# Seeding Strassen's second product in PSUM, a subtraction ahead of half of block 0's exponentials, and a new written order

## The chip, the cores and the metric

The kernel runs on one core of a Trainium2 chip. The metric is the device time of one execution in microseconds (us), lower is better. The engines are named as the profile names them: PE (TensorE, matrix products; its weight loads stand apart as PEld), DVE (VectorE), ACT (ScalarE), POOL (GpSimd) and SP (SyncE, which here only issues DMAs).

## The reference

An attention over pooled keys, and then a gated feed-forward layer on its output:

```
# q, k, v: (8, 8, 576, 64); keys and values are means over 8 neighbours, so 72 keys a head
scores = matmul(q, k_p.T) / sqrt(64)
scores = scores - max(scores)
attn   = exp(scores) / (sum(exp(scores)) + 1e-9)
x      = matmul(attn, v_p)  ->  reshaped to (4608, 512)
gate   = 1 / (1 + exp(-(x @ w_gate)))       # w_gate, w_val: (512, 1536)
out    = (gate * (x @ w_val)) @ w_out       # w_out: (1536, 512)
```

All of it is float32, to float32 accuracy.

## The kernel before, in words

The 4608 tokens are nine blocks of 512. A product is made in float32 accuracy from fp32r matmuls: each operand is split into a high and a low part (ACT casts the high part, DVE subtracts it to get the low one), and three matmuls take the place of one.

**Block 0** goes first, alone, in `first_pass`, beside the conversion of the weights (they arrive as float64 and are converted on ACT and DVE) and the attention of blocks 1 and 2. Each step of it is a word of the table `ORDER`; `exp.0.2.1`, for instance, is the exponential of block 0, pair of heads 2, half 1. For a pair and a half, `scores` fills a PSUM tile `sc` (128 queries x 4 x 72 keys), `maximum` takes the negated row maxima on DVE, and `exps` runs four ACT instructions of 72 columns, each with its own row maximum as bias and with a running sum (`accum_out`). The sums give 1/sum (`total`), the weighted values are transposed (tile `tp`), split and multiplied with the values (`av`), and become the operand `xo` of the feed-forward matmuls, whose PSUM tiles are called `chain` (x times w_gate or w_val) and `acc` (h times w_out).

**Blocks 1 to 8** go in four passes of two blocks each. In a pass, both large products use Strassen's method in Winograd's form, seven products m = 1 to 7 in place of eight. `product(kind, p, m)` makes one of them for the gate ("G") or the value ("V") of a pair p of columns: six matmuls of 128x512 into one of three PSUM banks, A, B or C, of that kind. Products 1, 6, 7 and 4 accumulate onto each other in bank A, product 5 and then 3 in bank C, and product 2 stands alone in bank B. After products 1, 5 and 6 ACT copies the bank to SBUF (tiles `sG` and `sV`), and after 2, 3 and 7 DVE adds that copy to the bank (tile `y`): result 0,0 is product 2 plus product 1. The gate's results go through a sigmoid on ACT (tile `gate`); the value's are multiplied with the gate on DVE (tile `h`). `second_sums` does the same for h times w_out with the tiles `acc`, `o` for results. There are 23 pairs in all, each for G and for V, and four second products of two banks each. While a pass multiplies, the attention of the next two blocks runs on the side; blocks 5 to 8 transpose through DRAM by POOL's DMAs (`turned`, `pt`, `pr`).

**The order** of all this is written out. The kernel's calls are only recorded, each as a unit (a group of matmuls that belong together is one unit), and the list `LATER` says in which order all units are issued. Every engine takes its instructions strictly as they stand in that list, so an instruction that waits holds up all that stand behind it on its engine. SP's DMAs have their place in the list too. All recorded instructions carry the line of the one call that issues them (L316), so the profile tells them apart by their tiles.

Of the kernel before, what the change touches and what calls it, by code (L numbers as in the profile page):

```python
# [11 lines left out]
F32 = mybir.dt.float32  # L12
# [3 lines left out]
AF = mybir.ActivationFunctionType  # L16
ALU = mybir.AluOpType
AX = mybir.AxisListType
# [40 lines left out]
BIASED = (3, 4)  # L59
TURNED = {5: ((0, 2), (2, 3), (3, 4)), 6: ((0, 3), (3, 4)), 7: ((0, 3), (3, 4)), 8: ((0, 4),)}  # L60
# [268 lines left out]
def attention_then_ffn(ctx: ExitStack, tc: tile.TileContext, qT, kT, vm, vr, vn, sums8, wgv, wo, const, out, outT):  # L329
# [518 lines left out]


    bank, seen, gates, hb = {}, {}, {}, {}  # L850

    def product(kind, p, m):

        b = {1: "A", 6: "A", 7: "A", 4: "A", 2: "B", 5: "C", 3: "C"}[m]
# [650 lines left out]
```

## Time and profile before

| | |
|---|---|
| time, median of 3 runs | 932.19 us (929.45 to 933.98) |
| the profiled execution | 925.95 us, of which 924.1 us from the first to the last instruction |
| busy in the span | PE 906.7, DVE 689.5, ACT 554.0, POOL 143.3 us |
| weight loads on PE | 741.0 us |
| granted TensorE clock | 0.998 in the mean |

Engines work beside each other, so their busy times don't add up. Only a wait of the engine that is full sets the end. Matmuls are pipelined, and the profile models their ends; a busy PE can hide a short wait. The profiled execution was quicker than the three timed ones.

### The profile page before, as it was taken

To read this page: it belongs to the slowest core of one execution; us is meant where nothing else is said; L and a number is where in the kernel's file an instruction comes from. 1 tells how busy PE (TensorE), PEld (TensorE's weight loads), DVE (VectorE), ACT (ScalarE), POOL (GpSimd) and SP (SyncE) were. 2 spreads that over 40 slices of the span, in tenths; PEclk is the share of its full clock that TensorE was granted. 3 is DMA by queue.
4 is the path that set the end of the run, shared out by engine and by line. 5 is a ranking of instruction groups with operands and counts; after the bars stand their busy time and mean duration, and the time that the engine had idled before them with its cause. 6 is when DMAs were issued, how large, how long until landed. Compare 5 with 4: busy or idle time off the path is not lost.

```text
span 924.1 us, 12611 instructions
## 1 busy us (share of the span) xinstructions
PE 906.7 (98%) x4188; PEld 741.0 (80%) x4188; DVE 689.5 (75%) x1086; ACT 554.0 (60%) x1178; POOL 143.3 (16%) x276
## 2 busy tenths in 40 slices
PE   7999999999999999999999999999999999999998
PEld 5677778878888888887888887888888888888886
DVE  5899989787879999874778988555688773343963
ACT  6999998888786774553546546343455362223442
POOL 1000000011211004424242424213222200000000
PEclk9999999999999999999999999999999999999999
DMA  9798886767785778886977786867646875565454
GB/s 323 268 319 290 296 324 260 257 222 273 286 291 193 254 227 287 264 281 220 329 264 248 232 298 220 265 227 243 225 155 226 246 243 190 205 222 205 172 180 155
DMA packets 96432, 228.38 MB, mean 247 GB/s; under 512 B 12784, under 2 KB 33136, under 8 KB 94832
## 3 DMA queue, kind: packets, MB, share of 16 engines
q1 hardware_dynamic: 83312, 197.68, 62.8%
q0 software_dynamic: 13056, 29.90, 9.7%
q8 instruction: 33, 0.54, 0.2%
q14 instruction: 31, 0.25, 0.1%
HBM read 171.43 MB, written 56.10 MB: 246 GB/s over the span
## 4 chain that ended last, share of the span: by engine, by line
PE 76%; DVE 6%; ACT 4%; DMA 1%; POOL 1%; issue 1%; DVEq 0%; ACTq 0%; SPq 0%; POOLq 0%
PE chain L316 45%; PE acc L316 24%; PE av L316 3%; PE sc L316 3%; POOL turned L316 1%; DVE hs L316 1%; DVE s L316 1%; ACT e L316 1%; DVE xo L316 1%; DMA parts<-keptV0C 1%; DVE h L316 1%; PE tp L316 1%; ACT L316 1%; ACT hs L316 0%; DMA turned<-turn 0%
## 5 line engine op out<-in xcount | busy, mean ns | idle before, releaser
L316 PE MATMUL chain<-xo,parts 128*128 128x512 f32 x2316 | 545.1, 392 | 2.7 <-DVE y L316 1.2
L316 PEld LDWEIGHTS chain<-xo,parts 128*128 128x128 f32 x2316 | 430.5, 188 | 97.1 <-DVE xo L316 2.4
L316 PE MATMUL acc<-hs,oparts 128*128 128x512 f32 x1008 | 238.3, 392 | 0.6 <-DVE hs L316 0.3
L316 PEld LDWEIGHTS acc<-hs,oparts 128*128 128x128 f32 x1008 | 187.3, 188 | 41.6 <-DVE hs L316 2.1
L316 POOL DMA_DIRECT2D turned<-turn x192 | 105.7, 553 | 249.3 <-DVE turn L316 153.6
L316 ACT COPY sG<-chain 128x512 f32<-128x512 f32 x69 | 39.9, 586 | 84.4 <-PE chain L316 84.2
L316 DVE TENSOR_TENSOR y<-chain,sG 128x512 f32<-128x512 f32 x69 | 47.0, 686 | 54.1 <-PE chain L316 32.4
L316 ACT CAST hs<-h 128x1024 fp32r<-128x1024 f32 x52 | 54.5, 1051 | 49.5 <-PE acc L316 39.6
L316 DVE TENSOR_TENSOR y<-chain,sV 128x512 f32<-128x512 f32 x69 | 47.1, 687 | 46.0 <-PE chain L316 31.6
L316 DVE TENSOR_TENSOR hs<-h,hs 128x1024 fp32r<-128x1024 f32 x52 | 63.1, 1218 | 12.1 <-ACT hs L316 11.9
L316 ACT COPY sV<-chain 128x512 f32<-128x512 f32 x69 | 39.7, 584 | 45.0 <-PE chain L316 43.2
L316 ACT CAST hs<-s 128x1024 fp32r<-128x1024 f32 x36 | 37.6, 1051 | 30.3 <-PE acc L316 10.4
L316 ACT ACTIVATE gate<-y 128x512 f32<-128x512 f32 x69 | 43.2, 632 | 17.8 <-DVE y L316 14.7
L316 DVE TENSOR_TENSOR h<-y,gate 128x512 f32<-128x512 f32 x69 | 46.7, 684 | 0.5
L316 DVE TENSOR_TENSOR hs<-s,hs 128x1024 fp32r<-128x1024 f32 x36 | 43.5, 1217 | 4.0 <-ACT hs L316 3.8
L316 ACT ACT_TABLE_LOAD x35 | 44.9, 1283 | 2.1 <-DVE h L316 1.1
L316 PE MATMUL sc<-kbd,raw 128*128 128x144 f32 (+1 forms) x262 | 41.7, 298 | 1.6 <-ACT e L316 1.1
L316 PEld LDWEIGHTS sc<-kbd,raw 128*128 128x128 f32 (+1 forms) x262 | 32.8, 176 | 11.3 <-issue 3.3
L316 PE MATMUL acc<-oparts,hs 128*128 128x512 f32 x144 | 40.9, 413 | 0.1
L316 DVE TENSOR_REDUCE m<-sc 128x4 f32<-128x288 f32 x48 | 21.7, 452 | 15.4 <-PE sc L316 15.2
L316 PEld LDWEIGHTS acc<-oparts,hs 128*128 128x128 f32 x144 | 26.6, 194 | 6.1 <-ACT oparts L316 0.5
L316 DVE TENSOR_TENSOR h<-chain,gate 128x512 f32<-128x512 f32 x23 | 15.8, 687 | 20.0 <-PE chain L316 16.6
(194 smaller groups left out, 1075.8 us busy)
## 6 DMA issues: line engine op xcount, KB each, us to landing
oparts<-keptS SPq DMA_DIRECT2D x48, 512.0 KB, 4.4
oparts<-keptO SPq DMA_DIRECT2D x72, 256.0 KB, 4.5
raw<-in_wgv SPq DMA_DIRECT2D x12, 1024.0 KB, 7.7
out<-o SPq DMA_DIRECT2D x36, 256.0 KB, 3.4
raw<-in_kT SPq DMA_DIRECT2D x28, 288.0 KB, 5.0
raw<-in_qT SPq DMA_DIRECT2D x29, 256.0 KB, 4.3
raw<-in_vm SPq DMA_DIRECT2D x24, 256.0 KB, 4.8
raw_o<-in_wo SPq DMA_DIRECT2D x12, 512.0 KB, 5.8
```

What stands on the lines that cost most here:

```text
L316: return self._book.take(lambda: f(*args, **named))
```

## The change

It has three parts. First, the second Strassen product no longer starts its own bank: after product 1 ACT copies bank A not to SBUF but to bank B, and product 2 accumulates onto that copy. The addition on DVE after product 2 goes away, the sigmoid or the multiplication reads the bank, and in `second_sums` the result of product 2 is copied out by ACT in place of an addition on DVE. Second, for pairs 2 and 3 of block 0 DVE adds the negated row maxima to the scores (288 columns), and ACT then takes one exponential of 576 columns for the pair; DVE sums its rows. Third, `LATER` is a new list.

```diff
+SUBBED = ((0, 2), (0, 3))
...
+    def chain_bank(kind, b):
+        return ps.tile([P, BT], F32, name="chain", tag=CHAIN["GV".index(kind) * 3 + "ABC".index(b)])
+
     def product(kind, p, m):
...
-        if m in (1, 2, 5):
-            bank[kind, b] = ps.tile([P, BT], F32, name="chain", tag=CHAIN["GV".index(kind) * 3 + "ABC".index(b)])
+        if m in (1, 5):
+            bank[kind, b] = chain_bank(kind, b)
...
-                        start=(m in (1, 2, 5) and c == 0 and k == 0), stop=(c == 1 and k == 2), skip_group_check=True,
+                        start=(m in (1, 5) and c == 0 and k == 0), stop=(c == 1 and k == 2), skip_group_check=True,
...
-        if m in (1, 5, 6):
+        if m == 1:
+            bank[kind, "B"] = chain_bank(kind, "B")
+            nc.scalar.copy(bank[kind, "B"], t)
+            return
+        if m in (5, 6):
...
-        if m != 4:
+        if m in (3, 7):
             y = two.tile([P, BT], F32, name="y", tag="y")
-            nc.vector.tensor_tensor(out=y, in0=t, in1=seen[kind, {2: 1, 3: 6, 7: 5}[m]], op=ALU.add)
+            nc.vector.tensor_tensor(out=y, in0=t, in1=seen[kind, {3: 6, 7: 5}[m]], op=ALU.add)
...
-                t = snap.tile([P, BT], F32, name="o", tag=f"sV{5 + c}")
+                t = snap.tile([P, BT], F32, name="o", tag=f"sV{5 + c}" if side else f"s{'GV'[c]}1")
...
-                    if m in (1, 5, 6):
+                    if m == 1:
+                        acc["B", c] = ps.tile([P, BT], F32, name="acc", tag=B_[c])
+                        nc.scalar.copy(acc["B", c], t)
+                    elif m in (5, 6):
...
-                        result(side, half, c, t, None if m == 4 else seen2[{2: 1, 3: 6, 7: 5}[m], c])
+                        result(side, half, c, t, None if m in (2, 4) else seen2[{3: 6, 7: 5}[m], c])
...
         def exps(j, p, hf):
             v = scs[j, p, hf].rearrange("p i (h k) -> p (i h) k", h=2)
+            e = es[p // 2][:, p % 2]
+            if (j, p) in SUBBED:
+                a = slice(QT * hf, QT * hf + QT)
+                m = maxima[j, p][:, a, None].broadcast_to([P, QT, KEYS])
+                nc.vector.tensor_tensor(out=e[:, a], in0=v, in1=m, op=ALU.add)
+                if p in subbed:
+                    nc.scalar.activation(e, e, AF.Exp)
+                    nc.vector.reduce_sum(out=totals[j, p // 2][:, p % 2], in_=e, axis=AX.X)
+                subbed.add(p)
+                return
```

The new list moves most instructions a little (a matmul by some ten places in the mean) and keeps the course of the work. It moves more at three places.

**ACT in block 0.** The rows below are ACT's at the exponentials of pairs 2 and 3 (tile `early`, 72 columns each before, 576 after); `vres` and `vh` are block 0's values, `w_241` and `raw_229` the first weights, `kbd` the keys. Before:

```order
L316 ACTIVATE early<-sc,early 128x72 x5
L316 CAST r_243<-rest 128x4x32
L316 ACTIVATE w_241<-raw_229 128x1024
L316 ACTIVATE raw_229<-raw_229,cst 128x1024
L316 ACTIVATE early<-sc,early 128x72 x4
L316 CAST early_211<-tp 128x512
L316 CAST ph<-tp 128x512
L316 ACTIVATE early<-sc,early 128x72 x7
```

And now:

```order
L315 ACTIVATE kbd_92<-early 64x72
L315 CAST vres_106<-vr 96x128
L315 ACTIVATE kbd_93<-early 64x72
L315 ACTIVATE early<-early 128x576
L315 CAST vres_107<-vr 96x128
L315 CAST vres_105<-vr 96x128
L315 CAST r_243<-rest 128x4x32
L315 ACTIVATE w_241<-raw_229 128x1024
L315 ACTIVATE raw_229<-raw_229,cst 128x1024
L315 CAST early_211<-tp 128x512
L315 ACTIVATE early<-early 128x576
L315 CAST ph<-tp 128x512
```

Sixteen short exponentials have become two, and the casts of the values have moved in between.

**SP at the start.** The rows are SP's first DMAs: `in_kT` and `in_qT` are keys and queries (288 and 256 KB), and `h_208` holds those of block 0; `raw_228` is a buffer for keys of block 1. Before:

```order
L316 DMA h_208<-in_kT 128x576
L316 DMA h_208<-in_qT 128x512
L316 DMA h_208<-in_kT 128x576 x2
L316 DMA h_208<-in_qT 128x512
L316 DMA cst_84<-in_const 128x133
L316 DMA h_208<-in_kT 128x576
```

And now:

```order
L315 DMA h_208<-in_kT 128x576 x2
L315 DMA h_208<-in_qT 128x512
L315 DMA h_208<-in_kT 128x576
L315 DMA h_208<-in_qT 128x512
L315 DMA raw_228<-in_kT 128x576
L315 DMA h_208<-in_qT 128x512
L315 DMA h_208<-in_kT 128x576
```

The first query comes one load of keys later, and a load for block 1 stands between block 0's.

**DVE in the third pass.** The rows are DVE's where block 5's attention comes back from its way through DRAM (`pl<-pt,ph`), beside pair 2 of the pass; `y<-chain,sV` are additions for the value, and the one with `sV_1022` before and `sV_990` now is that of product 7 of that pair. Before:

```order
L316 TENSOR_TENSOR y<-chain,sG_983 128x512
L316 TENSOR_TENSOR s_985<-w_984,s_985 128x256
L316 TENSOR_TENSOR y<-chain,sV_1004 128x512
L316 TENSOR_REDUCE ks<-raw 128x72
L316 TENSOR_TENSOR h<-y,gate_995 128x512
L316 TENSOR_TENSOR vl_101<-vs,vh_96 64x64
L316 TENSOR_TENSOR s_985<-w_984,s_985 128x256
L316 TENSOR_TENSOR pl<-pt,ph 128x512
L316 TENSOR_REDUCE vs<-raw 128x64
L316 TENSOR_TENSOR pm<-e,rz 128x512
L316 TENSOR_TENSOR e<-sc,m 128x288
L316 TENSOR_TENSOR y<-chain,sV_1022 128x512
```

And now:

```order
L315 TENSOR_REDUCE ks<-raw 128x72
L315 TENSOR_TENSOR vl_101<-vs,vh_96 64x64
L315 TENSOR_TENSOR y<-chain,sG_962 128x512
L315 TENSOR_TENSOR y<-chain,sV_990 128x512
L315 TENSOR_TENSOR y<-chain,sV_995 128x512
L315 TENSOR_TENSOR h<-y,gate_963 128x512
L315 TENSOR_TENSOR pl<-pt,ph 128x512
L315 TENSOR_TENSOR vl_101<-vs,vh_96 64x64
L315 TENSOR_TENSOR h<-chain,gate_963 128x512
L315 TENSOR_TENSOR pm<-e,rz 128x512
```

Product 2's addition is gone (its multiplication reads `chain`, behind `pl`), and the additions of products 7 and 3 have moved ahead of `pl`.

## Rows read from the trace of the kernel before

**Rows 1.** The page: each engine's busy us, share of the span, instructions.

```profile
PE 906.7 (98%) x4188; PEld 741.0 (80%) x4188; DVE 689.5 (75%) x1086; ACT 554.0 (60%) x1178; POOL 143.3 (16%) x276
```

**Rows 2.** Windows over five stretches: length, then busy time of PE, PEld, DVE, ACT, POOL.

```profile
0.00:24.00 24.00, 17.22 (x57) 13.28 (x58) 13.01 (x27) 17.02 (x81) 2.49 (x20) 1.00 0.87 311
24.00:42.00 18.00, 16.00 (x75) 11.10 (x73) 15.04 (x33) 16.14 (x35) 0.00 (x0) 1.00 0.79 257
42.00:126.00 84.00, 81.33 (x392) 64.23 (x392) 75.92 (x132) 80.47 (x213) 0.00 (x0) 0.98 0.85 304
126.00:921.00 795.00, 792.12 (x3668) 652.41 (x3666) 585.55 (x896) 440.23 (x852) 140.79 (x256) 1.00 0.71 239
921.00:924.10 3.10, 0.00 (x0) 0.00 (x0) 0.00 (x0) 0.12 (x1) 0.00 (x0) 1.00 0.44 169
```

**Rows 3.** Windows, same columns: a stretch in which PE never idles.

```profile
750.00:900.00 150.00, 150.00 (x662) 123.56 (x661) 78.64 (x95) 56.87 (x86) 0.00 (x0) 1.00 0.58 195
```

**Rows 4.** The chain of work that ended last, one piece in that stretch.

```profile
753.73 107.79 PE chain L316 x474
```

**Rows 5.** Timeline of PE in the first 60 us: start, us, what, count.

```profile
5.05 4.57 PE L316 MATMUL sc<-kbd,h 128*128 128x144 f32 x16 [5.05 <-ACT kbd L316]
...
56.94 0.65 PE L316 MATMUL sc<-kbd,raws 128*128 128x144 f32 x4
```

**Rows 6.** Who PE waited for: total us, times, longest us.

```profile
PE chain L316 <- DVE y L316: 1.2, 1, 1.2
PE sc L316 <- ACT e L316: 1.1, 2, 0.8
PE tr L316 <- ACT r L316: 0.8, 1, 0.8
PE av L316 <- DVE early L316: 0.4, 1, 0.4
```

**Rows 7.** Groups of instructions by shape: busy us, mean ns, idle before.

```profile
L316 DVE TENSOR_TENSOR y<-chain,sV 128x512 f32<-128x512 f32 x69 | 47.1, 687 | 46.0 <-PE chain L316 31.6 <-ACT gate L316 10.3 <-ACT sV L316 3.5
L316 DVE TENSOR_TENSOR e<-sc,m 128x288 f32<-128x288 f32 x32 | 14.5, 453 | 0.8
L316 DVE TENSOR_REDUCE ks<-raw 128x72 f32<-128x576 f32 x20 | 14.8, 741 | 0.2 <-DMA raw<-in_kT 0.2
L316 ACT COPY sG<-chain 128x512 f32<-128x512 f32 x69 | 39.9, 586 | 84.4 <-PE chain L316 84.2
L316 ACT ACTIVATE gate<-y 128x512 f32<-128x512 f32 x69 | 43.2, 632 | 17.8 <-DVE y L316 14.7 <-DVE h L316 2.6
L316 ACT ACTIVATE e<-e 128x1152 f32<-128x1152 f32 x8 | 9.4, 1169 | 1.1 <-DVE e L316 1.0
```

**Rows 8.** Timeline of DVE, then of PE, at 425 to 436 us.

```profile
431.27 0.69 DVE L316 TENSOR_TENSOR pl<-pt,ph 128x512 fp32r<-128x512 f32 x1 [5.18 <-DMA pr<-turned]
...
433.57 0.68 DVE L316 TENSOR_TENSOR y<-chain,sV 128x512 f32<-128x512 f32 x1
...
434.30 1.66 PE L316 MATMUL chain<-xo,parts 128*128 128x512 f32 x6 [1.19 <-DVE y L316]
```

**Rows 9.** Timeline of ACT in block 0's exponentials.

```profile
17.27 0.32 ACT L316 ACTIVATE early<-sc,early 128x72 f32<-128x72 f32 x1
...
17.56 0.33 ACT L316 ACTIVATE early<-sc,early 128x72 f32<-128x72 f32 x1
```

**Rows 10.** Timeline of DVE: the first two loads of keys arrive.

```profile
3.56 0.75 DVE L316 TENSOR_REDUCE early<-h 128x72 f32<-128x576 f32 x1 [3.56 <-DMA h<-in_kT]
5.79 0.75 DVE L316 TENSOR_REDUCE early<-h 128x72 f32<-128x576 f32 x1 [1.47 <-DMA h<-in_kT]
```

**Rows 11.** Tile `xo`, 28 to 42 us: durations (min/median/max), first and last start.

```profile
L316 PE MATMUL chain<-xo,parts x24: 386/395/504, 31.5 to 41.8; 128*128 128x512 f32 x24
```

**Rows 12.** Windows around 116 us; the granted clock follows POOL.

```profile
116.00:118.00 2.00, 1.98 (x8) 1.83 (x9) 1.97 (x6) 1.98 (x10) 0.00 (x0) 0.69 0.99 414
118.00:120.00 2.00, 2.00 (x7) 1.50 (x7) 1.74 (x3) 2.00 (x12) 0.00 (x0) 0.50 0.51 205
```

More of the change, by code (lines that the diff above doesn't have):

```diff
@@ L1078, in second_sums @@
                     for c in range(2):
-                        if i % 3 == 0 and k == 0 and m in (1, 2, 5):
+                        if i % 3 == 0 and k == 0 and m in (1, 5):
                             acc[name, c] = ps.tile([P, BT], F32, name="acc", tag={"A": A, "B": B_, "C": C}[name][c])
@@ L1083, in second_sums @@
                                 acc[name, c], lhsT=w[:, k, h, c * P:(c + 1) * P], rhs=hs[:, y, k],
-                                start=(m in (1, 2, 5) and i % 3 == 0 and k == 0 and t == 0), stop=(i % 3 == 2 and k == 1 and t == 2),
+                                start=(m in (1, 5) and i % 3 == 0 and k == 0 and t == 0), stop=(i % 3 == 2 and k == 1 and t == 2),
                                 skip_group_check=True,
@@ L1208, in maximum @@
             nc.vector.reduce_max(out=maxima[j, p][:, QT * hf:QT * hf + QT], in_=v, axis=AX.X, negate=True)
+        subbed = set()
         def exps(j, p, hf):
             v = scs[j, p, hf].rearrange("p i (h k) -> p (i h) k", h=2)
+            e = es[p // 2][:, p % 2]
[8 more added lines that the diff above has]
+                return
             for i in range(QT):
@@ L1214, in exps @@
                 nc.scalar.activation(
-                    es[p // 2][:, p % 2, k], v[:, i], AF.Exp, bias=maxima[j, p][:, k:k + 1],
+                    e[:, k], v[:, i], AF.Exp, bias=maxima[j, p][:, k:k + 1],
                     accum_out=totals[j, p // 2][:, p % 2, k:k + 1],
@@ L1277, in sum_v @@
                         )
-            for i in range(4):
-                a = 240 + 24 - KR * i
-                nc.tensor.matmul(
-                    vp["r"][:, :, i], lhsT=got["U0"][:D, a:a + 96],
-                    rhs=got["R0"][:D].rearrange("p (g a d) -> p g a d", a=4, d=D)[:, :, i], start=True, stop=True,
-                )
+            with book.unit():
+                for i in range(4):
+                    a = 240 + 24 - KR * i
+                    nc.tensor.matmul(
+                        vp["r"][:, :, i], lhsT=got["U0"][:D, a:a + 96],
+                        rhs=got["R0"][:D].rearrange("p (g a d) -> p g a d", a=4, d=D)[:, :, i], start=True, stop=True,
+                    )
         def of_v(p):
```

308 rows, old and new, of the table LATER are left out of this document.

## The prediction

> **What bounds the kernel now.** I read the page first. PE is busy for 906.7 of 924.1 us and every other engine for at most 75% [rows 1]. So the first question is where PE still waits, and the windows answer it stretch by stretch [rows 2]. From 0 to 24 us PE is busy for 17.22 us, from 24 to 42 for 16.00 of 18, from 42 to 126 for 81.33 of 84, from 126 to 921 for 792.12 of 795, and the last 3.1 us are the copy and the store after the last matmul. PE's idle time is then 6.78, 2.00, 2.67, 2.88 and 3.10 us, together 17.4 us. Nothing that DVE or ACT is spared can bring more than what they are the cause of here.
>
> A busy PE may hide short waits, so I look at a second measure. From 750 to 900 us PE does not idle at all, and its weight loads fill 123.56 of 150 us, 82.4% [rows 3]; there 474 matmuls follow each other in 107.79 us, 227 ns apiece [rows 4]. If PE were as dense elsewhere, the loads of 126 to 921 us (652.41) would need 652.41 / 0.824 = 791.8 us of 795, so 3.2 us are lost there, about what the idle time says. Those of 42 to 126 us (64.23) would need 77.9 of 84, so 6.1 us are lost there against 2.67 idle. I take this as the outer bound, since the small score matmuls of that stretch have another share of loads.
>
> The Trainium skill (Perfetto Trace Analysis, Identifying the Most-Contended Engine) says that a matmul's busy share is no good measure of headroom and that the weight loads' busy share is one. By the busy row the whole span could give back 17.4 us, by the loads 924.1 - 741.0 / 0.824 = 24.8 us. In the long stretch after 126 us the two agree here.
>
> Next, who PE waits for. In the order of the program: its first matmul, at 5.05 us, waits for ACT's first keys [rows 5]. Later its longest waits are 0.8 us for ACT's `r`, 1.1 us in two waits for ACT's exponentials (the longer one 0.8), 0.4 us for DVE behind them, and 1.2 us for a DVE addition `y` [rows 6]. The waits for ACT lie before 126 us, all but the shorter of those two, and there ACT is full: 80.47 of 84 us, against 75.92 for DVE. After 126 us ACT has 440 of 795 and DVE 586 of 795 [rows 2]. So two different engines can hold PE up: ACT before 126 us, DVE after.
>
> **Part 1, the seed.** Each of the 46 products 2 (23 pairs, G and V) loses its addition on DVE, 0.687 us each [rows 7], and the eight results of product 2 in `second_sums` lose theirs, for which I take the same price: 54 x 0.687 = 37.1 us less DVE. ACT copies as often as before after product 1, only to PSUM. No row shows an ACT copy into PSUM; the nearest is the copy from PSUM to SBUF, 0.586 us [rows 7]. Were it dearer or cheaper by a fifth, 54 of them would shift ACT by 6 us over a stretch in which it idles for 355, so I cost it at nothing, and the cover is that idle time. ACT also takes eight more result copies, 8 x 0.586 = 4.7 us, under the same cover. The sigmoid of product 2 reads a bank in place of `y`, also under it.
>
> The new wait is product 2's for the seed. It has little to bite on: product 6 accumulates onto bank A and had to wait for the same copy of product 1 before the change. In the new list at least six matmuls stand between the last of product 1 and the first of product 2 (four of the 46 have only six), and six take 6 x 0.227 = 1.36 us against a copy of 0.586. So the wait stays hidden as long as ACT comes to the copy within 0.7 us. Behind it on PE would stand everything.
>
> What are 37 us of DVE worth? DVE's work is not on the path as a sum; it counts where something stands behind DVE. One place shows it: at 426 us DVE idles 5.18 us at `pl`, which waits for block 5's way through DRAM; the addition of product 7 stands three rows further, runs at 433.57, and PE, which needs the bank for product 4, starts 1.19 us late [rows 8]. In the new list this addition stands ahead of `pl`. I expect that wait to go. The rest of the 2.88 us after 126 us are small pieces. I take **-2 us** for this stretch; the bounds are 0 (other small waits take their place) and -3.2.
>
> **Part 2, the exponentials.** A short exponential with its running sum starts every 0.29 us [rows 9]; 16 are 4.7 us of ACT. Two of 576 columns take their place. Between 512 columns at 0.632 and 1152 at 1.169 us one is 0.69 us by a straight line [rows 7], so 1.4 us, and ACT is spared 3.3 us. DVE gets four subtractions of 288 columns at 0.453 us and two sums over 576 at 0.741 us [rows 7], 3.3 us more. Both lie on the way from the scores of pairs 2 and 3 to their weighted values, so this way gets hardly shorter: what ACT gives, DVE takes. It costs little that it is DVE, which has 13.01 of the first 24 us busy against ACT's 17.02 [rows 2].
>
> **Part 3, the order at the start.** The first two loads of keys arrive 2.2 us apart, at 3.56 and 5.79 us, with the first query between them in the queue [rows 10]. The query now stands third, so it arrives about where the second keys did, and the first matmul starts at some 5.8 in place of 5.05 us [rows 5]: +0.7 us. Against it, ACT reaches everything behind the exponentials about 3 us sooner, the casts of the values that `av` needs among them. And the new list lets all `av` of block 0 run ahead of the first `chain` matmul, so PE has work while the operand is still being split. To compare like with like I use the moment at which the 24th `chain` matmul starts, 41.8 us before [rows 11]. PE idles 2.00 us between 24 and 42 us [rows 2], and about half of that could go. The sum: +0.7, -1 to -2 for the idle time, nothing for part 2. I take **-1 us**; the bounds are -3.5 (ACT's 3.3 us in full) and +3.5 (DVE's 3.3 us in full on the way, nothing gained).
>
> **Part 4, from 42 to 126 us.** ACT is the full engine here and arrives about 3 us ahead with its work, and PE's waits for it in this stretch are 0.8 + 0.8 + 0.4 = 2.0 us [rows 6]. After the last two of them the granted clock fell: 0.69 from 116 to 118 us and 0.50, the level of 1.2 GHz, from 118 to 120 [rows 12]. That cost 2 x 0.31 + 2 x 0.50 = 1.6 us. If the waits go, the fall goes too. Together 3.6 us can be had where the cause is ACT. I take **-3 us**; the bounds are 0 (DVE, at 75.92 of 84 us plus what part 2 adds, takes over as the full engine) and -6.1, from the loads.
>
> The Trainium skill (TensorE: Matmul & The Clock Gate, Part 1: The HAM clock gate) has the low clock as the gate's default, which activity releases. The rows around 116 us agree: the level fell after PE had idled. The granted clock reads 1.00 in the first 24 us, though, and the rows of matmuls there don't fit that: four score matmuls of the first kind take a quarter of 4.57 us, 1.14, against 0.65 later [rows 5]; by the rule they ran at the low level.
>
> **The sum.** -1 - 3 - 2 = -6 us. The profiled execution's own time is 925.95 us (924.1 of span and 1.85 around it), so it would take 919.95. The three timed runs have their median 6.2 us above that execution, and I expect the same of the changed kernel's: 932.2 - 6 = **926.2 us**.
>
> **The rivals.** (a) *The spared work was off the path.* DVE idles a quarter of the span, and PE's few waits move to other places with the new list: for it speaks that 792.12 of 795 us are already full; against it that the waits before 126 us have one cause, ACT, which is relieved. With parts 3 and 4 at -1 together and the rest 0 it gives 931. (b) *The start gets longer.* This is the other sign. Pairs 2 and 3 now go from PSUM to DVE, to ACT, and to DVE again, where weight conversions of 1.2 us stand between; if PE runs dry between the transposes and `av`, its matmuls stay at the low level, as those of the first 24 us were. Then 14 `av` and 24 `chain` matmuls at twice 227 ns cost 38 x 0.227 = 8.6 us more. With that and the waits after it half gone (-2.5) the time is 938. It decides when the 24th `chain` matmul starts later than 41.8 + 5 = 46.8 us. For it speaks the longer way and the later first query, against it that PE now has more work without `chain` before that. (c) *The seed comes late.* If ACT stands in a cast of 1 us when product 1 ends, each such product 2 or 6 waits; this bites only where six matmuls lie between, 12 times in the new list, so even 0.5 us each is 6 us and eats the gain: 932. That the list doesn't do what it says is no rival, since the instructions can be counted.
>
> **How the numbers follow.** The forecast has a chance of 0.52, (a) 0.30, (b) 0.11, (c) 0.07. The best sum of bounds is -3.5 - 6.1 - 3.2 = -12.8 us, 919.4; the worst single case is (b), 938. Medians of three runs of this kernel can lie 2 us apart, and 0.5% (4.7 us) is about what its measurement can tell from no change. The range from 918 to 935 leaves out one in ten on the slow side and less on the fast. Faster than 927.5 is most of the forecast and a little of (a): 0.50. Slower than 936.9 is most of (b) and the tail of (c): 0.12. Within lies 0.38.
>
> **What would show it.** Right: the window from 42 to 126 us has its work done 3 to 5 us sooner, no fall of the granted clock near 116 us, no wait for `y` near 430, DVE's busy time near 656 us, PE's near 903. Wrong: the 24th `chain` matmul only after 44 us (part 3), PE waiting for ACT's copies into `chain` (the seed), or DVE nearly full before 126 us and PE waiting for it (part 4). The forecast falls if PE's idle time in the new profile adds up to 15 us or more.

## The result and the profile after

The changed kernel takes 921.18 us (median of 4 runs, 920.07 to 924.49) against 931.83 us (4 runs, 929.45 to 933.98) for the kernel before, run beside it. The ratio is 0.9892, with a 95% interval from 0.9856 to 0.9928: 10.65 us less. The forecast was 926.2 in a range from 918 to 935, and faster by over 0.5%.

The two profiles shown hide most of this. The profiled execution of before (925.95 us) was quicker than all four of these runs, that of the changed kernel (924.49) the slowest of its four. So the changed kernel was run and profiled once more (the run `c1_changed_again` below, a profiled execution of 919.98 us, a median of 923.36), and both of its profiles stand here.

The page, engines, first profile of the changed kernel:

```profile
PE 900.5 (98%) x4188; PEld 738.2 (80%) x4188; DVE 656.8 (71%) x1038; ACT 554.6 (60%) x1156; POOL 143.2 (16%) x276
```

DVE has lost 32.7 us against [rows 1], ACT has the same sum. PE, which does the same matmuls, is busy for 6.2 us less; the windows show that 4.4 of these lie in the first 24 us (12.81 against 17.22 in [rows 2], with 70 matmuls on record for 57).

Windows, first profile, columns as in [rows 2]; the last two stretches are cut where the shorter of the two profiles ends:

```profile
0.00:24.00 24.00, 12.81 (x70) 11.00 (x70) 16.61 (x40) 17.41 (x64) 2.49 (x20) 0.99 0.94 348
24.00:42.00 18.00, 17.68 (x76) 14.25 (x76) 17.40 (x30) 17.18 (x35) 0.00 (x0) 0.82 0.75 251
42.00:126.00 84.00, 81.33 (x400) 64.70 (x399) 76.42 (x135) 80.64 (x220) 0.00 (x0) 1.00 0.91 318
126.00:915.00 789.00, 784.86 (x3629) 645.47 (x3629) 546.32 (x835) 438.22 (x840) 140.67 (x256) 1.00 0.70 239
```

And of the second profile:

```profile
42.00:126.00 84.00, 82.20 (x403) 65.65 (x402) 77.61 (x137) 81.74 (x223) 0.00 (x0) 1.00 0.91 320
126.00:915.00 789.00, 786.73 (x3639) 646.93 (x3637) 544.87 (x832) 437.67 (x837) 140.70 (x256) 1.00 0.71 238
```

From 42 to 126 us the granted clock is whole in both; the fall of [rows 12] is gone. After 126 us PE idles for 4.14 us in the first and 2.27 in the second. What differs between the two is named by the view of who PE waited for after 126 us, first profile:

```profile
PE av L315 <- DMA pr<-turned: 0.9, 1, 0.9
PE acc L315 <- DMA oparts<-keptS: 0.8, 1, 0.8
PE sc L315 <- DVE e L315: 0.7, 1, 0.7
```

None of these three is listed in the second profile, where the longest wait after 126 us is 0.4 us. The first two are transfers that come late in one execution and not in the next. In neither profile is a wait of PE for ACT's copies into `chain` listed, nor one for a `y`. Only its weight loads wait for these copies; the row is the same in both profiles:

```profile
PEld chain L315 <- ACT chain L315: 1.6, 5, 0.5
```

The mark for the start is the 24th `chain` matmul, as in [rows 11]. The tile `xo`, first profile, 26 to 38.6 us, then second, 26 to 38.1:

```profile
L315 PE MATMUL chain<-xo,parts x24: 387/389/487, 33.2 to 38.5; 128*128 128x512 f32 x24
```

```profile
L315 PE MATMUL chain<-xo,parts x24: 387/390/487, 32.7 to 38.1; 128*128 128x512 f32 x24
```

It comes at 38.5 and 38.1 us in place of 41.8. The first of these matmuls is later than before (33.2 against 31.5), but then they run without a gap.

A second mark stands further on, near the end of the stretch from 42 to 126 us: the 527th matmul, the first of 48 `chain` matmuls in a row. In every execution profiled here 130 matmuls lie up to the first mark and 396 between it and the second, the same in kind and number, so both marks compare like with like. PE's timeline of before, of the first and of the second profile:

```profile
126.70 11.15 PE L316 MATMUL chain<-xo,parts 128*128 128x512 f32 x48
```

```profile
120.70 12.11 PE L315 MATMUL chain<-xo,parts 128*128 128x512 f32 x48 [0.93 <-ACT parts L315]
119.26 12.10 PE L315 MATMUL chain<-xo,parts 128*128 128x512 f32 x48
```

It comes 6.0 and 7.4 us sooner.

The groups that answer to [rows 7], first profile:

```profile
L315 ACT COPY chain<-chain 128x512 f32<-128x512 f32 x46 | 26.5, 577 | 60.6 <-PE chain L315 49.2 <-DVE h L315 11.4
L315 ACT COPY sG<-chain 128x512 f32<-128x512 f32 x46 | 26.9, 587 | 48.8 <-PE chain L315 48.7
L315 ACT ACTIVATE gate<-chain 128x512 f32<-128x512 f32 x46 | 26.9, 596 | 10.5 <-PE chain L315 9.1 <-DVE sums L315 0.8 <-DVE h L315 0.5
```

The seed's copy costs 577 ns, the copy to SBUF 587. A sigmoid that reads the bank takes 596 ns, one that read `y` took 632 [rows 7]. The Trainium skill (Perfetto Trace Analysis, Optimizing Scalar/DVE Operations) has ACT's access to PSUM cheaper than that to SBUF, by 42 ns an instruction; the 36 ns here come near it.

### The profile page after: what moved, and what is told of

Its sections match the earlier page's. It is cut to its first block, busy times and chain, and to the rows that moved or that the text cites. A ratio compares the mean times of both kernels' runs of the same rounds, so it can differ in the third digit from the quotient of the medians.

```text
span 922.4 us, 12567 instructions
## 1 busy us (share of the span) xinstructions
PE 900.5 (98%) x4188; PEld 738.2 (80%) x4188; DVE 656.8 (71%) x1038; ACT 554.6 (60%) x1156; POOL 143.2 (16%) x276
## 4 chain that ended last, share of the span: by engine, by line
PE 80%; ACT 5%; DMA 5%; DVE 4%; POOL 2%; issue 1%; SPq 0%; DVEq 0%; POOLq 0%; ACTq 0%
PE chain L315 48%; PE acc L315 24%; PE av L315 4%; PE sc L315 3%; POOL turned L315 2%; DMA raw<-in_wgv 1%; DMA turned<-turn 1%; PE tp L315 1%; DMA oparts<-keptS 1%; DMA parts<-keptG2C 1%; ACT early L315 1%; DMA pr<-turned 1%; ACT w L315 1%; ACT raw L315 1%; DVE early L315 1%
## 5 line engine op out<-in xcount | busy, mean ns | idle before, releaser
L315 DVE TENSOR_TENSOR y<-chain,sV 128x512 f32<-128x512 f32 x46 | 31.6, 688 | 71.0 <-PE chain L315 52.2
L315 ACT COPY chain<-chain 128x512 f32<-128x512 f32 x46 | 26.5, 577 | 60.6 <-PE chain L315 49.2
L315 DVE TENSOR_TENSOR y<-chain,sG 128x512 f32<-128x512 f32 x46 | 31.2, 686 | 36.6 <-PE chain L315 23.6
L315 ACT COPY sG<-chain 128x512 f32<-128x512 f32 x46 | 26.9, 587 | 48.8 <-PE chain L315 48.7
L315 DVE TENSOR_TENSOR h<-chain,gate 128x512 f32<-128x512 f32 x46 | 31.0, 683 | 22.8 <-PE chain L315 21.8
L315 ACT COPY sV<-chain 128x512 f32<-128x512 f32 x46 | 26.5, 584 | 28.7 <-PE chain L315 28.6
L315 PE MATMUL acc<-oparts,hs 128*128 128x512 f32 x144 | 38.7, 404 | 0.0
L315 ACT ACTIVATE gate<-y 128x512 f32<-128x512 f32 x46 | 28.6, 631 | 11.2 <-DVE y L315 11.0
L315 ACT ACTIVATE gate<-chain 128x512 f32<-128x512 f32 x46 | 26.9, 596 | 10.5 <-PE chain L315 9.1
L315 DVE TENSOR_TENSOR h<-y,gate 128x512 f32<-128x512 f32 x46 | 31.4, 682 | 0.5 <-ACT gate L315 0.3
```

What stands on the lines that cost most here:

```text
L315: return self._book.take(lambda: f(*args, **named))
```

## The experiments

Each kernel was timed against the kernel before, run beside it. Four things can be told apart: the seed, the exponentials, and the new list in two stretches, the start (up to the first Strassen product) and the passes. The theory was that most of the gain lies in the start, through the order and ACT's relief; the rivals were that the 37 us of DVE in the passes are the gain, or the list alone.

### One part at a time

**The seed in the old order.** The changed kernel with `SUBBED = ()`, and every instruction where the old list has it. Six of the 46 products 2 stood ahead of their product 1 in the old list, and three directly behind it. The seed forbids the first, so 21 units had to leave their places. In the order that was run nine of the 46 stand directly behind their product 1, with no matmul between to cover the copy.

```diff
-SUBBED = ((0, 2), (0, 3))
+SUBBED = ()
...
-LATER = the new list
+LATER = the old list
```

> The seed alone: products 2 accumulate onto ACT's copy, their 54 additions on DVE are gone; the short exponentials stay, and every instruction stands where the old list has it, apart from 21 places where the new data need another order. Theory (the gain comes from the new order and from ACT's relief before 126 us): 929 to 933 us against about 932 of before, ratio 0.997 to 1.001; DVE's busy time falls by about 37 us all the same. Rival (the 37 us of DVE are the gain): 922 to 925 us, ratio 0.990 to 0.993.

Measured: 978.43 us against 930.43, ratio 1.0521 (1.0477 to 1.0566). It lies 45 us above the nearer of the two expectations. Who PE waited for, after 126 us:

```profile
PE chain L315 <- ACT chain L315: 21.1, 15, 3.6
PE chain L315 <- ACT xo L315: 5.0, 2, 3.4
PE chain L315 <- ACT gate L315: 4.1, 4, 2.0
```

The seed comes late, the third rival of the prediction. One of the 15 waits, ACT's timeline and then PE's:

```profile
214.87 0.58 ACT L315 COPY sG<-chain 128x512 f32<-128x512 f32 x1
215.35 0.32 ACT L315 ACTIVATE e<-sc,m 128x72 f32<-128x72 f32 x1
...
216.10 0.19 ACT L315 ACTIVATION_READ_ACCUMULATOR e<-sc,m 128x1 f32 x1
216.19 0.58 ACT L315 COPY chain<-chain 128x512 f32<-128x512 f32 x1
```

```profile
216.83 3.02 PE L315 MATMUL chain<-xo,parts 128*128 128x512 f32 x12 [3.37 <-ACT chain L315]
```

The copy stands behind the next blocks' short exponentials; in the kernel before it was not needed until product 6. Product 2 waits 3.37 us for it. DVE is spared its 33 us here too (656.7 us busy) and the kernel is 48 us slower. The waits for the seed are 21.1 us of this; the rest was not taken apart.

**The exponentials in the old order.** The kernel before with the new `exps`; the subtractions stand where the first of the short exponentials stood, the long exponentials and their sums where the last did. Nothing else moves.

```diff
+            if (j, p) in SUBBED:
...
+                nc.vector.tensor_tensor(out=e[:, a], in0=v, in1=m, op=ALU.add)
+                if p in subbed:
+                    nc.scalar.activation(e, e, AF.Exp)
```

> The subtraction ahead of two long exponentials alone, in the old order, without the seed. Theory: ACT is 3.3 us freer in a stretch where it is full, so 929 to 931 us, and PE's progress at 126 us is 1 to 3 us ahead of before. Rival (what ACT gives, DVE takes, and the spared work was off the path): 931 to 933, ratio 0.999 to 1.001.

Measured: 932.64 us against 930.43, ratio 1.0029 (1.0006 to 1.0053). No gain, and rather a small loss, as the rival had it. PE's progress is not ahead either: the 527th matmul starts at 131.2 us.

**Both edits in the old order.** The changed kernel with the old list.

```diff
-LATER = the new list
+LATER = the old list
```

> Both edits of the computation in the old order, apart from 21 places. Theory (part of the gain from the edits before 126 us, most from the order): 928 to 930 us. Rival (the edits themselves are the gain, whatever the order): 921 to 923 us, ratio 0.989 to 0.991.

Measured: 980.85 us, ratio 1.0555 (1.0506 to 1.0603), as the seed alone.

**The new list without the edits.** The kernel before with the new list. The 46 additions and eight results of product 2 had to be given places of my own choice, so this bounds the list's worth from one side only.

```diff
-LATER = the old list
+LATER = the new list
```

> Neither edit, only the new list: the old instructions stand where the changed kernel's stand; the additions of products 2 are put two thirds of the way from the product to the instruction that uses the sum, the short exponentials where the subtractions and the long exponentials stand. Theory (the order is most of the gain): 923 to 927 us, ratio 0.991 to 0.996, with the first 126 us at least 3 us shorter. Rival (the order was fitted to the edits and brings nothing without them): 930 us or more, ratio 0.998 or more.

Measured: 977.53 us, ratio 1.0509 (1.0469 to 1.0550). PE waits after 126 us, the first row:

```profile
PE chain L316 <- DVE y L316: 12.5, 8, 3.0
```

The loss lies in the passes: the 527th matmul starts at 120.6 us, 6.1 us sooner than in the profile of before, so the part of the theory on the first 126 us holds without either edit.

The four runs together say that seed and list belong to each other in the passes: either alone, in the orders tried, costs 47 to 48 us. So part for part the passes were not taken apart, and the next runs cut by time in place of by edit, with whole orders on each side of the cut.

### Cut at the first Strassen product

**New start, old passes.** The changed order and exponentials up to the first product, then the kernel before; no seed. Twelve instructions cross the seam. The expectations put this product near 126 us, where the prediction's windows part; it starts at 190 us. The first products for G and V in PE's timeline of before:

```profile
190.04 3.03 PE L316 MATMUL chain<-xo,parts 128*128 128x512 f32 x12
```

```diff
-LATER = the old list
+LATER = the new list up to the first product, the rest by the old list
```

> The changed kernel up to the first Strassen product (about 126 us: its order and its exponentials), from there the kernel before: no seed, the old order. Twelve instructions are moved across the seam. Theory (most of the gain arises in the first 126 us): 924 to 927 us against about 931 of before, with the first pass starting 3 to 7 us earlier. Rival (the gain arises in the passes, by the seed with an order fitted to it): 929 to 931 us, what is won at the start being lost again by 250 us.

Measured: 925.00 us against 931.59, ratio 0.9918 (0.9892 to 0.9943): -6.6 us. The theory holds, with the 527th matmul at 119.3 us.

**Old start, new passes.** The reverse: the kernel before up to the first product, then seed and new list.

```diff
-SUBBED = ((0, 2), (0, 3))
+SUBBED = ()
...
-LATER = the new list
+LATER = the old list up to the first product, the rest by the new list
```

> The kernel before up to the first Strassen product, from there the changed kernel: the seed and its order. Ten instructions are moved across the seam. Theory (most of the gain arises in the first 126 us): 926 to 930 us. Rival (the passes are the gain): 921 to 924 us, with PE's waits after 126 us under 2 us in sum. A third case, that the passes of the new list bring a loss without the new start: over 932 us.

Measured: 930.24 us, ratio 0.9979 (0.9962 to 0.9996): -1.35 us, at the edge of the theory's range and far from the rival's. The two cuts add up to -7.9 us, against the changed kernel's -10.65 and -8.5 in its two measurements.

**The changed kernel with short exponentials.** Seed and new list stay.

```diff
-SUBBED = ((0, 2), (0, 3))
+SUBBED = ()
```

> The changed kernel without the subtraction: the sixteen short exponentials stand where the subtractions (first half of a pair) and the long exponentials (second half) stand; seed and new order stay. Theory (ACT's relief in block 0 is worth its 3.3 us, where ACT is full): 923 to 925 us. Rival (what ACT gives, DVE takes): 920 to 922 us, as the changed kernel.

Measured: 924.50 us, ratio 0.9910 (0.9887 to 0.9933). The interval holds the changed kernel's ratio too, so the time alone settles nothing; the mark does, below.

**The first query ahead of the second keys.** SP's rows, changed kernel and this one:

```
 L315 DMA h_208<-in_kT 128x576
-L315 DMA h_208<-in_kT 128x576
 L315 DMA h_208<-in_qT 128x512
+L315 DMA h_208<-in_kT 128x576
```

> The changed kernel with one thing undone: on SP's queue the first query goes ahead of the second load of keys again, as before. Theory (the start is on the path: the first matmul comes at about 5.1 in place of 6.4 us, and the rest follows): 919.5 to 920.5 us. Rival (the start of the first score matmuls is covered by what comes later): 921 to 922 us, as the changed kernel.

Measured: 923.94 us, ratio 0.9906 (0.9876 to 0.9936). The changed kernel's first profile and then this one, PE's timeline: the first score matmul comes 1.3 us sooner, and PE then waits for the next query.

```profile
6.42 2.02 PE L315 MATMUL sc<-kbd,h 128*128 128x144 f32 x7 [6.42 <-DMA h<-in_qT]
```

```profile
5.12 2.26 PE L315 MATMUL sc<-kbd,h 128*128 128x144 f32 x8 [5.12 <-ACT kbd L315]
7.93 0.58 PE L315 MATMUL sc<-kbd,h 128*128 128x144 f32 x1 [0.56 <-DMA h<-in_qT]
```

The time lies above both ranges, but so does the changed kernel when it is run again (923.36, below). No gain can be told, and the 24th `chain` matmul starts at 37.9 us, against 38.5 and 38.1 of the changed kernel: the rival holds, most of the 1.3 us is covered.

### What the start is worth, and what one addition is worth

**The changed kernel again**, as the measure for the other three.

> The changed kernel once more, with nothing changed, as the measure for the runs beside it: 920 to 924 us. If it lies at 923 to 924, the first query ahead of the second keys (923.94 in its run) made no difference; if it lies at 920 to 921, that order is 3 us worse, against what its start promised.

Measured: 923.36 us against 931.87, ratio 0.9908 (0.9884 to 0.9933).

**The order at the start alone.** The new list up to the first product, old passes, short exponentials, no seed: the kernel before with

```diff
-LATER = the old list
+LATER = the new list up to the first product, the rest by the old list
```

> The new list up to the first Strassen product and the kernel before from there, with neither edit: the sixteen short exponentials stay, at the places of the subtractions and the long ones. Theory (of the 6.6 us that the new start gave, about 3 come from ACT's relief by the long exponentials, the rest from the order): 927 to 929 us. Rival (the order alone does it): 924 to 926 us, as with the long exponentials.

Measured: 928.32 us, ratio 0.9964 (0.9949 to 0.9980): -3.55 us, where the same with the long exponentials gave -6.6: the theory holds. The marks say more, since they leave out the passes. The 24th `chain` matmul of this kernel, and of the new start with long exponentials:

```profile
L316 PE MATMUL chain<-xo,parts x24: 387/393/487, 34.6 to 40.1; 128*128 128x512 f32 x24
```

```profile
L317 PE MATMUL chain<-xo,parts x24: 387/389/489, 32.5 to 37.9; 128*128 128x512 f32 x24
```

Both marks in all executions profiled, in us, each cell sorted:

| | short exponentials | long exponentials |
|---|---|---|
| 24th `chain`, old start | 38.2, 39.6, 41.8, 42.7 | 42.0, 43.5 |
| 24th `chain`, new start | 39.5, 40.1, 40.1 | 37.6, 37.9, 37.9, 38.1, 38.5 |
| 527th matmul, old start | 123.9, 124.6, 126.7, 130.8 | 127.2, 131.2 |
| 527th matmul, new start | 120.6, 121.0, 121.4 | 118.8, 119.3, 119.3, 119.8, 120.7 |
| between the two, old start | 84.9, 85.0, 85.7, 88.1 | 85.2, 87.7 |
| between the two, new start | 80.9, 81.1, 81.3 | 80.9, 81.2, 81.4, 82.2, 82.2 |

At the first mark the long exponentials are worth 2 us in the new order; in the old one they show no gain (42.0 and 43.5 against a scatter from 38.2 to 42.7). The old start scatters by 4.5 us there where the new one scatters by 0.9, so the 41.8 of [rows 11] is one draw. Between the marks the new order is about 4 us shorter, with short exponentials as with long, and in the old order the long ones save nothing. So in this stretch the order is the gain, and not ACT's spared 3.3 us. PE's longest waits say the same, from 43 to 118 us: the old order with long exponentials, then the new order with short ones (before, [rows 6], has 0.8 and 0.8).

```profile
PE tr L317 <- ACT r L317: 1.9, 1, 1.9
PE sc L317 <- ACT e L317: 1.0, 2, 0.8
```

```profile
PE tr L316 <- ACT r L316: 0.7, 1, 0.7
PE sc L316 <- ACT e L316: 0.4, 1, 0.4
```

**One addition moved.** The kernel before, with one DVE instruction moved. DVE's rows:

```
-L316 TENSOR_TENSOR pl<-pt,ph 128x512
-L316 TENSOR_REDUCE vs<-raw 128x64
-L316 TENSOR_TENSOR pm<-e,rz 128x512
-L316 TENSOR_TENSOR e<-sc,m 128x288
 L316 TENSOR_TENSOR y<-chain,sV_1022 128x512
+L316 TENSOR_TENSOR pl<-pt,ph 128x512
+L316 TENSOR_REDUCE vs<-raw 128x64
+L316 TENSOR_TENSOR pm<-e,rz 128x512
+L316 TENSOR_TENSOR e<-sc,m 128x288
```

> The kernel before with one instruction of DVE moved: the addition of product 7 goes ahead of the subtraction that waits for block 5's way through DRAM, in the third pass. Theory (PE's wait for that addition, 1.2 us in the profile of before and 3.4 us in that of the subtraction alone, is a real loss of the old passes): 928 to 930 us, ratio 0.996 to 0.999, and no wait for y. Rival (the next instruction then waits for the same transfer, and PE for it): 930.5 to 932 us.

Measured: 929.11 us, ratio 0.9962 (0.9945 to 0.9980): -2.76 us for one row, as the theory had it. DVE's timeline:

```profile
433.49 0.69 DVE L316 TENSOR_TENSOR y<-chain,sV 128x512 f32<-128x512 f32 x1 [3.04 <-PE chain L316]
438.12 0.69 DVE L316 TENSOR_TENSOR pl<-pt,ph 128x512 fp32r<-128x512 f32 x1 [3.94 <-ACT ph L316]
```

The addition runs as soon as product 7 is done, and `pl` waits 3.94 us behind it; no wait of PE for a `y` is listed any more. The place in three other kernels that keep the old passes, PE's timeline: the new start with long exponentials, with short ones, and the old start with the new exponentials:

```profile
430.09 1.66 PE L317 MATMUL chain<-xo,parts 128*128 128x512 f32 x6 [1.79 <-DVE y L317]
```

```profile
434.59 2.92 PE L316 MATMUL chain<-xo,parts 128*128 128x512 f32 x6 [3.69 <-DVE y L316]
```

```profile
440.94 2.93 PE L317 MATMUL chain<-xo,parts 128*128 128x512 f32 x6 [3.43 <-DVE y L317]
```

The wait is 1.19 [rows 8], 1.79, 3.69 and 3.43 us, by how late the transfer is. After the long ones the next six matmuls also take 2.9 us in place of 1.66. The granted clock fell; windows of the new start with short exponentials:

```profile
434.00:436.00 2.00, 1.41 (x3) 1.16 (x4) 1.14 (x2) 0.00 (x0) 0.00 (x0) 0.66 0.89 344
436.00:438.00 2.00, 2.00 (x7) 1.67 (x6) 0.45 (x1) 0.00 (x0) 0.00 (x0) 0.50 0.11 45
```

**New start and that addition, without the seed.** The kernel of new start and old passes, with one unit of its list moved:

```
+L317 y<-chain,sV, the addition of product 7 (pair 2 of the third pass, value)
 L317 pl<-pt,ph, block 5
 ...
-L317 y<-chain,sV, the addition of product 7
```

> The new start with the passes of before, and the same one instruction of DVE moved in them; no seed. Theory (start and that wait are nearly all of the gain): 922 to 924 us, within 2 us of the changed kernel. Rival (the seed brings more in the passes than that one wait): 925 us as with the new start alone, and 3 us or more above the changed kernel.

Measured: 921.38 us against 931.87, ratio 0.9890 (0.9865 to 0.9915), beside 923.36 and 0.9908 for the changed kernel on the same chip. The two can't be told apart, and this one has no seed. Against the new start alone (0.9918, on another chip) the one row again brings some 3 us, though the two intervals overlap. Its profiled execution was its slowest (930.32), through one wait of 4.01 us for ACT's `sV` at 640 us. ACT had stood there at a cast that waits for a block's way through DRAM:

```profile
638.45 0.62 ACT L317 CAST ph<-pt 128x512 fp32r<-128x512 f32 x1 [7.56 <-DMA turned<-turn]
638.97 0.59 ACT L317 ACTIVATE gate<-chain 128x512 f32<-128x512 f32 x1
639.46 0.58 ACT L317 COPY sV<-chain 128x512 f32<-128x512 f32 x1
```

It is the same pattern on another engine: a copy that PE needs, queued behind a transfer of changing length.

## Why the prediction was right, and where its terms were off

**The sum.** Forecast -6 us, measured -10.65 and -8.5. The time lies in the range, and direction and places were right: most of the gain comes ahead of 126 us, the rest at one addition. But the first term was too small, and the second came by another cause than the one given.

**The start, -1 us: this term was too small.** The 24th `chain` matmul came 3.3 us sooner in the first profile and 3.7 in the second, near the bound that the prediction had named (-3.5). The step that failed is the sentence on part 2, "what ACT gives, DVE takes". In the old order it holds (932.64 us, 0.3% slower). In the new order the long exponentials bring the mark from 40 to 38 us. The list puts the casts of the values into the time that ACT gains; that the 2 us arise in this way is read from the list and not tested. And the old start's 41.8 us, from which the term was counted, was taken for a fixed time, where it scatters by 4.5 us. The penalty of +0.7 us for the first query came (+1.4 at the first matmul) and was without effect, as the run with the query first shows.

**From 42 to 126 us, -3 us: right in size, not in cause.** The prediction had ACT arrive 3 us ahead through the spared exponentials. The new order without them is as short between the marks (80.9 to 81.3 us) as with them, and the old order with them is no shorter than without (85.2 and 87.7 against 84.9 to 88.1). So the new list is the cause; which of its moves does it was not tried, and the waits that the profiles list, with the fall of the clock, account for some 2 of the 4 us. That the size came out is in part luck. The fall of the clock, put at 1.6 us, was no fixed cost either: between 100 and 128 us it shows in three of the six old starts profiled and in none of the eight new ones, and in the three without it PE waits for the same instructions. For start and this stretch together the forecast was -4; the 527th matmul came 6.0 and 7.4 us sooner, and the run with the new start alone gave -6.6. Two readings were off as well: of the 2.0 us of waits put down to ACT 0.4 are for DVE [rows 6], and the list of waits left out 1.0 us in two waits for DVE's `xo`, at 32 and 40 us.

**After 126 us, -2 us: right in place and size.** The prediction tied the term to one addition behind `pl`, and moving that row alone gave -2.76 us (-5.1 to -1.9). The profile of before had shown the wait at its shortest of four, 1.19 us. The seed with its new list gave -1.35 us (-3.5 to -0.4). The profiles alone would have misled here: from the 527th matmul to the end of the span the changed kernel needs 4.3 us more than before in its first profile and 1.4 more in its second (922.4 - 120.7 and 918.1 - 119.3 against 924.1 - 126.7).

**The seed costs nothing that can be told, and is worth little.** In both profiles of the changed kernel PE waits for none of the 46 copies, as forecast, though five of its weight loads do, for at most 0.5 us; with the old start it waits once, for 1.3 us. The 33 us that it spares DVE bought nothing that can be told: the kernel without it, with one row moved, is as fast. That DVE's sum was not on the path, rival (a), was true of the sum; the forecast rested on the row, and the row was the gain.

**The rivals.** (a) at 931 fell with the start. (b), the longer start, did not come: the mark is earlier. (It counted 14 `av`; 16 stand there.) But a part of its mechanism is there. The granted clock of the changed kernel reads 0.82 from 24 to 42 us, and its first `av` matmuls run at the lower level; windows of the first profile:

```profile
26.00:28.00 2.00, 2.00 (x8) 1.61 (x7) 2.00 (x5) 1.90 (x3) 0.00 (x0) 0.50 1.03 398
28.00:30.00 2.00, 2.00 (x6) 1.61 (x5) 1.88 (x5) 2.00 (x4) 0.00 (x0) 0.50 0.49 191
```

PE had waited 2.3 us for DVE's `r` some 3 us before, its timeline says:

```profile
23.34 0.41 PE L315 MATMUL tp<-cst,early 128*128 128x128 f32 x2 [2.32 <-DVE r L315]
```

The gain was made in spite of this, and what it costs was not tried. (c), the late seed, is no idle fear: where the list isn't made for it PE waits 21.1 us for it, in a kernel that is 48 us slower, against the 6 us that the prediction had put on it.

**The step to the median.** The prediction added to the changed kernel the 6.2 us by which the median of before lay above its profile. That worked by luck: one profile was at the quick end of its spread, the other at the slow end of its own, and the difference of the two spans, 1.7 us, was a sixth of the difference of the medians.

## What to carry to other kernels

An engine takes its instructions in order, so nothing that the bounding engine needs soon should stand behind one that waits for a transfer of changing length: one such row was worth 2.8 us of 932, and 33 us of work taken off the same engine brought nothing beyond that. An edit that adds a dependence and the order that leaves room for it are one change; tried apart, in the orders chosen here, either cost 5%, and a cut by time told what each stretch was worth. A term whose size comes out has not shown its cause: the same edit in the old order, and the new order without it, did that here. Where two profiled executions differ by as much as the effect, take marks inside the program with the same work ahead of them, and the medians of several runs for the rest.

## What the runs showed of the hardware

An early row of the granted clock may not be the clock. From 16 to 24 us the kernel before, the one with one addition moved and the one with the old start and new passes do the same work; their windows, in this order:

```profile
16.00:24.00 8.00, 8.00 (x26) 5.30 (x25) 5.25 (x9) 5.97 (x28) 0.00 (x0) 1.00 0.81 325
```

```profile
16.00:24.00 8.00, 8.00 (x26) 5.29 (x25) 5.25 (x9) 5.96 (x28) 0.00 (x0) 0.50 0.79 317
```

```profile
16.00:24.00 8.00, 8.00 (x31) 6.70 (x31) 6.18 (x12) 6.81 (x30) 0.00 (x0) 0.60 0.81 322
```

The same 26 matmuls fill the same 8.00 us under 1.00 and under 0.50. So before was at the low level there as well, as the prediction had suspected from the pace of its score matmuls. In the third the clock rose within the stretch (0.60), and its mark comes 3.1 us before the second's (39.6 against 42.7): the early rise goes with the early mark. What sets it stays open.

A short wait of PE can cost more than itself: 1.79 us left the next six matmuls at 1.66 us, 3.69 us let the granted clock fall to 0.50, and the six took 2.92. The length of one wait doesn't settle it: at 116 us the clock of the kernel before fell [rows 12] behind waits of 0.84 and 0.43 us.
